# Chunk low parts moved from GpSimd to VectorE, and one more large product or two behind each phase's first count

## The chip, the core and the metric

The program runs on one core of a Trainium2 chip. Five engines work side by side, each through its own queue in order: TensorE (PE in the profile, with its weight loads as PEld), VectorE (DVE), ScalarE (ACT), GpSimd (POOL) and SyncE (SP, which only issues transfers here). They wait for one another through semaphores. The metric is the device time of one launch in microseconds; less is better. A difference of 0.2% (1.8 us) is about what a measurement of this kernel can tell from none.

## The reference

Three layers in a row: decayed causal attention over 4 x 8 heads of 576 tokens, a leaky feed-forward layer over all 2304 tokens, and an expert layer in which each of 8 experts takes exactly 288 tokens. Which expert a token goes to is decided by a greedy walk over all 18432 logits, largest first. Cut to what matters here:

```python
# second layer
h = x @ w_in                      # 2304 x 512 by 512 x 2048
g = np.maximum(0.01 * h, h)
x = g @ w_out                     # "the second product": 2304 x 2048 by 2048 x 512
# third layer
logits = x @ w_gate               # 2304 x 8
order = np.argsort(-logits.flatten())
for idx in order:                 # a token takes the first expert in the order that has room
    tok, e = int(idx) // E, int(idx) % E
    if assigned[tok] >= 0 or counts[e] >= cap: continue
    assigned[tok] = e; counts[e] += 1
out[mask_e] = np.maximum(x[mask_e] @ w1[e], 0) @ w2[e]      # for each expert e
```

## The kernel before

The kernel runs in stages. The first 190 us or so are attention. Up to about 440 us TensorE makes the first product of the leaky layer, twice over half of its 2048 columns, and the gate's logits with it. From 440 us to 659 us two things share TensorE, and the change is there. From 659 us the rows of the first expert are gathered, and from 675 us the eight experts run.

**What shares TensorE from 440 us.** `deferred` (L976) is a generator that gives out the second product, one matmul at a time. It goes over nine groups `g` of 256 tokens; in a group over eight chunks, each of which is two 128-row blocks of the inner 2048. fp32 operands are split into a high and a low part, both read as fp32r, and a product is the sum of three matmuls: high by high, high by the weight's low part, low by high. A chunk is thus 12 matmuls of 128x128 by 128x512 ("large products" below), a group 96, all of it 864. `taken` (L990) fetches a chunk, a tile `g1` that is still in SBUF or a tile `g0` read back from memory, and `split_g` (L454) makes the parts: `gh` is a cast on ScalarE (L458), `gl` a subtraction (L459). Each has three buffers, so ScalarE can write `gh` of a chunk once TensorE is through with the chunk three before it. For groups 0 to 7 `gl` is made on GpSimd; in the last group the first two chunks are on VectorE, and the rest on VectorE in a fixed order.

`routing` (L1256) is the greedy walk, done as a threshold search. It has seven phases of the same form, 0 to 6, and a last one that only assigns. In a phase VectorE first brings the state up to date and forms each token's wish `r_oh` (about twenty small instructions, L1391 to L1338, called the update below). Then five counts follow, three for the high digits of the threshold and two for the low ones. A count is: VectorE compares every token's key with 127 or 63 candidates (`r_ge`, L1358), TensorE adds up the results by expert (18 small matmuls into `q_ct`), VectorE reads them and marks which candidates hold (L1367, L1368: `r_found`), and TensorE sums the marks into the next base (`q_base`, one or more tiny matmuls), which the next `r_ge` reads as its scalar. After the counts, two small matmuls into `q_misc` give totals, and the next update begins.

**What sets the order.** TensorE's order is written out by the loop at L1119 to L1123. `routing` yields a number of nanoseconds each time that it has to wait for VectorE; the loop adds PACE (1.05) times that number to `slack` and lets `deferred` give out one large product for each 228 ns of it. `deal` later gives out the rest: up to the 852nd before the first expert's rows are turned (L1140), and the last 12 behind them. On TensorE everything stands in program order. On VectorE and ScalarE the instructions called by `V` and `A` are placed by a scheduler, those by `vec` and `act` stay in program order.

**The end of the stage.** When all is assigned, three groups of six small matmuls into `q_misc` (L1452) turn the assignment into row numbers `ids`. GpSimd then issues three indirect transfers that gather the first expert's rows (`xe`, L1034, 96 rows of 2 KB each). TensorE goes on with large products up to the 852nd, then turns the gathered rows by 36 small matmuls (L1143), 12 for each of the three gathers, into `q_ct`, `q_base` and `q_misc`. With the trace's 817 large products given out by the last of the three groups, 35 lie between it and the turning.

GpSimd has other work in that stage: per phase four small updates (L1406 to L1409), and for groups 3 and 4 the low parts of the first expert's weights (L988 through L366, printed as L75: `wh`, two instructions each time).

## Time and profile before

| | |
|---|---|
| median of 3 runs | 907.79 us (907.22 to 908.92) |
| the profiled execution | 908.27 us, of which the span of the instructions is 906.5 us |
| TensorE busy in the span | 879.0 us (97%) |
| VectorE / ScalarE / GpSimd busy | 583.2 / 413.1 / 439.1 us |
| granted TensorE clock, mean | 0.993 |

The page's busy times say which engine is the one that the others must keep fed; the waits say where it was not. A matmul's end is modelled, so a row's duration overlaps the next row: two large products that follow one another start 0.23 us apart though each is printed with 0.39 us. Where TensorE waits, the start of the waiting row tells more than the idle time printed beside it.

### The profile page before, as it was taken

Reading aid. Unit: us, or ns where it says so; the run is one execution under the profiler, and the core shown is the slowest. Engines: PE = TensorE matmul, PEld = TensorE weight load, DVE = VectorE, ACT = ScalarE, POOL = GpSimd, SP = SyncE. Lnnn points to the kernel's source line nnn. Section 1 sums busy time; section 2 is a strip of 40 time slices with the busy share of each in tenths; the row PEclk is TensorE's granted clock in tenths of the full one; section 3 lists DMA queues with packets and bytes.
Section 4 is the critical chain, followed back from the end, with each engine's and each line's share of the span. In section 5 each row is a group of like instructions: output and inputs, shape, how many; then the busy total and the mean of one; then the engine's idle time right before and its main releaser. Section 6 shows DMA issues by size and latency. Waiting matters only on the chain.

```text
span 906.5 us, 18991 instructions
## 1 busy us (share of the span) xinstructions
PE 879.0 (97%) x6916; PEld 749.3 (83%) x6916; DVE 583.2 (64%) x1456; ACT 413.1 (46%) x986; POOL 439.1 (48%) x670
## 2 busy tenths in 40 slices
PE   6899999999999999999999999999999999999996
PEld 5688888877778887777777777777789999999995
DVE  8778776617789369524576767767755666666651
ACT  7999999852223223323222222222244545554541
POOL 8488895456999158200464666565122122221111
PEclk9899999999999999999999999999999999999998
DMA  6556655559985484431121321111247666665521
GB/s 130 149 159 167 179 144 129 145 165 350 326 284 175 151 230 139 154 94 47 56 85 60 93 82 59 59 63 55 71 148 219 206 195 204 186 197 177 186 88 35
DMA packets 139964, 132.33 MB, mean 146 GB/s; under 512 B 68480, under 2 KB 106688, under 8 KB 139872
## 3 DMA queue, kind: packets, MB, share of 16 engines
q1 hardware_dynamic: 135600, 121.40, 44.1%
q0 software_dynamic: 3072, 9.44, 3.6%
q8 instruction: 54, 0.88, 0.4%
q10 hardware_dynamic: 1200, 0.30, 0.2%
q14 instruction: 38, 0.31, 0.1%
HBM read 99.84 MB, written 31.08 MB: 144 GB/s over the span
## 4 chain that ended last, share of the span: by engine, by line
PE 78%; POOL 8%; issue 4%; DVE 3%; ACT 3%; DMA 2%; POOLq 0%; SPq 0%; ACTq 0%; DVEq 0%
PE acc L1112 21%; PE acc L75 11%; PE h L75 11%; PE y L1197 10%; PE h L1184 9%; PE s L75 7%; PE T L75 3%; POOL wsq L75 3%; PE q_ct L1112 2%; ACT kept L75 2%; POOL ln L75 2%; DVE r_ge L1358 1%; POOL wst L75 1%; DMA w<-in_moe_w_in 1%; PE T L1204 1%
## 5 line engine op out<-in xcount | busy, mean ns | idle before, releaser
L1112 PE MATMUL acc<-wh,gh 128*128 128x512 f32 x568 | 184.5, 400 | 0.0
L459 POOL TENSOR_TENSOR gl<-g,gh 128x512 fp32r<-128x512 f32 x63 | 104.8, 1669 | 77.8 <-ACT gh L458 74.2
L1112 PEld LDWEIGHTS acc<-wh,gh 128*128 128x128 f32 x568 | 105.1, 189 | 18.6
L1112 PE MATMUL acc<-wh,gl 128*128 128x512 f32 x284 | 113.3, 399 | 0.0
L458 ACT CAST gh<-g 128x512 fp32r<-128x512 f32 x65 | 40.2, 621 | 145.8 <-PE acc L1112 135.6
L75 PE MATMUL acc<-X,wh 128*128 128x512 f32 (+1 forms) x480 | 104.6, 374 | 0.7 <-issue 0.7
L1197 PE MATMUL y<-eh,wh 128*128 128x288 f32 x512 | 104.3, 297 | 0.0
L75 PE MATMUL h<-X,wh 128*128 128x512 f32 (+1 forms) x480 | 104.3, 374 | 0.0
L1184 PE MATMUL h<-XE,wh 128*128 128x288 f32 x660 | 100.7, 299 | 0.0
L75 PEld LDWEIGHTS acc<-X,wh 128*128 128x128 f32 x480 | 82.5, 188 | 19.1 <-issue 2.1
L75 PEld LDWEIGHTS h<-X,wh 128*128 128x128 f32 x480 | 82.5, 188 | 17.5 <-issue 1.2
L1184 PEld LDWEIGHTS h<-XE,wh 128*128 128x128 f32 x660 | 89.8, 188 | 0.0
L75 ACT ACTIVATE kept<-kept,nm 128x192 f32<-128x192 f32 (+4 forms) x160 | 88.0, 553 | 3.1 <-DVE nm L75 3.1
L1210 POOL DMA_INDIRECT out<-yo,ids x24 | 22.5, 936 | 124.5 <-DVE yo L1206 98.3
L1197 PEld LDWEIGHTS y<-eh,wh 128*128 128x128 f32 x512 | 82.0, 188 | 0.0
L75 DVE TENSOR_TENSOR wh<-ws,wh 128x512 fp32r<-128x512 f32 x116 | 75.6, 687 | 2.5
L1189 DVE SCALAR_TENSOR_TENSOR el<-h,eh 128x288 fp32r<-128x288 f32 x64 | 29.2, 457 | 73.5 <-ACT eh L1188 73.5
L1197 PE MATMUL y<-el,wh 128*128 128x288 f32 x256 | 74.6, 297 | 0.0
L75 DVE SCALAR_TENSOR_TENSOR wbits<-w,wbits 128x256 int32<-128x256 int32 x128 | 72.6, 569 | 2.3
L75 DVE CUSTOM_DVE_ANT_0 kept<-s,mask 128x192 f32<-128x192 f32 (+4 forms) x160 | 59.2, 426 | 23.0 <-PE s L75 22.0
L75 POOL TENSOR_TENSOR wst<-wsq,wbits 128x256 f32<-128x256 f32 x64 | 50.6, 791 | 34.3 <-DVE wbits L75 29.6
L1188 ACT ACTIVATE eh<-h 128x288 fp32r<-128x288 f32 x64 | 26.3, 411 | 89.5 <-PE h L1184 77.6
(252 smaller groups left out, 1801.5 us busy)
## 6 DMA issues: line engine op xcount, KB each, us to landing
ws<-in_moe_w SPq DMA_DIRECT2D x116, 256.0 KB
X<-xd SPq DMA_DIRECT2D x12, 1024.0 KB
g<-gd SPq DMA_DIRECT2D x36, 256.0 KB
w<-in_moe_w_in SPq DMA_DIRECT2D x32, 256.0 KB
w<-in_moe_w_out SPq DMA_DIRECT2D x32, 256.0 KB
gd<-g SPq DMA_DIRECT2D x16, 512.0 KB
xd<-xt SPq DMA_DIRECT2D x16, 320.0 KB
x2d<-xo SPq DMA_DIRECT2D x20, 256.0 KB
```

The costliest lines, as they stand in the source:

```text
L75: r = getattr(self.engine, name)(*a, **k)
L458: hi_on.copy(gh, g)
L459: on.tensor_tensor(gl, g, gh, op=OP.subtract)
L1112: tc.keep_in_program_order(PE.matmul(*a, **k))
L1184: (pe if own else PE).matmul(h[:, :CAP], w[:, 128 * (j % 4):128 * (j % 4) + 128], X[:, c, x, :], start=n == 0, stop=n == 3 * NC - 1)
L1188: A.activation(gh, h[:, :CAP], AF.Relu)
L1189: V.scalar_tensor_tensor(gl, h[:, :CAP], 0.0, gh, op0=OP.max, op1=OP.subtract)
L1197: o = PE.matmul(yt[c][:, :CAP], w[:, s], a, start=j == 0 and n == 0, stop=j == NJ - 1 and n == 2)
L1204: PE.transpose(p[:M, 128 * c:128 * c + 128], ys[:, c, M * t:M * t + M], ident)
L1210: sd = G.indirect_dma_start(out=out[:, :], out_offset=bass.IndirectOffsetOnAxis(ap=ids[:, 3 * e + t:3 * e + t + 1], axis=0), in_=y, in_off ...
L1358: V.scalar_tensor_tensor(many[:, :NT * (K + 1)].rearrange("p (i k) -> p i k", k=K + 1)[:, :, :K], key[:, :, None].to_broadcast(s), base if ...
```

## The change

Two edits, of one line each. In `taken`, the low part `gl` of a chunk of groups 0 to 7 is called on `V` (VectorE, placed by the scheduler) instead of `G` (GpSimd); the last group is as before. In `routing`, the yield ahead of the first count's last base product (`half == n == 0`) grows from 550 to 850.

```diff
                 n = NF // 2 * half + i
-                return split_g(x, *((vec, act) if g == NG - 1 and n > 1 else (V if g == NG - 1 else G, A)))
+                return split_g(x, *((vec, act) if g == NG - 1 and n > 1 else (V, A)))
             ahead = begun if g == 0 else []
...
                 V.tensor_scalar(found[:, n:n + 1], most, 0.0, stp, op0=OP.is_ge, op1=OP.mult)
-                yield 550
+                yield 550 + 300 * (half == n == 0)
                 mm(base, rows[K], found[:, n:n + 1], start=n == 0, stop=True)
```

63 subtractions change engine. The 300 ns come once in each of seven phases: 300 x 1.05 / 228 = 1.38 large products each time, 9.7 in all. The count of large products given out by the last group of `q_misc` goes from 817 to 827, and so 25 instead of 35 are left up to the turning.

VectorE, the first count of phase 2 (`r_step_6152` are the 127 candidates; `g_...` is the chunk that is read). Before:

```order
L1336 TENSOR_TENSOR r_mw<-r_mw,r_U 128x18
L1358 SCALAR_TENSOR_TENSOR r_ge<-r_kf,r_step_6152 128x18x127
L1338 TENSOR_TENSOR r_oh<-r_mw,r_we 128x144
L1367 ISA r_jk,r_most<-q_ct,r_nr 128x8
L1367 ISA r_most 128x1
L1368 TENSOR_SCALAR r_found<-r_most 128x1
```

And in the changed kernel:

```order
L1336 TENSOR_TENSOR r_mw<-r_mw,r_U 128x18
L1358 SCALAR_TENSOR_TENSOR r_ge<-r_kf,r_step_6152 128x18x127
L459 TENSOR_TENSOR gl<-g_6944,gh 128x512
L1338 TENSOR_TENSOR r_oh<-r_mw,r_we 128x144
L459 TENSOR_TENSOR gl<-g_6988,gh 128x512
L459 TENSOR_TENSOR gl<-g_7033,gh 128x512
L1367 ISA r_jk,r_most<-q_ct,r_nr 128x8
```

Three low parts stand behind the 127-wide compare, ahead of the count's reading; a fourth stands in the update ahead of these rows. The first of the three, of chunk 21, is read by the 255th large product.

VectorE, the third count of phase 0 (`r_step_6156` are 63 candidates). Before:

```order
L1358 SCALAR_TENSOR_TENSOR r_ge<-r_kf,q_base,r_step_6156 128x18x63
L1367 ISA r_jk,r_most<-q_ct,r_nr 128x8
L1367 ISA r_most 128x1
L1368 TENSOR_SCALAR r_found<-r_most 128x1
L1374 TENSOR_SCALAR r_k_6367<-r_kf,q_base 128x18
```

And in the changed kernel:

```order
L1358 SCALAR_TENSOR_TENSOR r_ge<-r_kf,q_base,r_step_6156 128x18x63
L1367 ISA r_jk,r_most<-q_ct,r_nr 128x8
L1367 ISA r_most 128x1
L459 TENSOR_TENSOR gl<-g_6426,gh 128x512
L1368 TENSOR_SCALAR r_found<-r_most 128x1
L1374 TENSOR_SCALAR r_k_6369<-r_kf,q_base 128x18
```

A low part has come between the reading of the count and its mark, in this count alone.

GpSimd, one piece of the difference, from the small updates behind phase 1's counts to those behind phase 2's (`wh` are the weights' low parts):

```order
 L75 TENSOR_TENSOR wh<-wst,wh 128x512 x2
-L459 TENSOR_TENSOR gl<-g_5606,gh 128x512 x4
-L459 TENSOR_TENSOR gl<-g_7246,gh 128x512
-L1407 TENSOR_SCALAR r_nr<-r_rp 128x8
-L1408 TENSOR_SCALAR r_r<-r_rp 128x8
-L1409 TENSOR_TENSOR r_nr<-r_nr,r_r 128x8
-L1406 TENSOR_TENSOR r_A<-r_A,r_asg 128x144
-L459 TENSOR_TENSOR gl<-g_7285,gh 128x512
-L459 TENSOR_TENSOR gl<-g_7303,gh 128x512
-L459 TENSOR_TENSOR gl<-g_7370,gh 128x512
+L1406 TENSOR_TENSOR r_A<-r_A,r_asg 128x144
+L1407 TENSOR_SCALAR r_nr<-r_rp 128x8
```

The low parts are gone from GpSimd, and each pair of `wh` has moved up: before it stood among the low parts of a phase's counts, now between L1409 and L1406, that is in the update that leads to phase 2 (the second pair: to phase 3).

## Rows read from the trace of the kernel before

**Rows 1.** The page, busy time of an engine, share of the span, instructions.

```profile
PE 879.0 (97%) x6916; PEld 749.3 (83%) x6916; DVE 583.2 (64%) x1456; ACT 413.1 (46%) x986; POOL 439.1 (48%) x670
```

**Rows 2.** Stretch: length, busy of each engine, granted clock, DMA share, GB/s.

```profile
370.00:590.00 220.00, 218.01 (x1431) 164.86 (x1430) 130.91 (x292) 54.78 (x93) 93.18 (x91) 1.00 0.23 73
```

**Rows 3.** Waits of TensorE from 430 to 680 us: total, times, longest.

```profile
PE q_ct L1112 <- DVE r_ge L1358: 2.2, 6, 0.8
```

**Rows 4.** Groups by line, within 370 to 620 and 439 to 660 us.

```profile
L459 POOL TENSOR_TENSOR gl<-g,gh 128x512 fp32r<-128x512 f32 x57 | 95.3, 1678 | 68.1 <-ACT gh L458 64.9 <-DVE W L75 1.9 <-PE acc L1112 1.2
L1358 DVE SCALAR_TENSOR_TENSOR r_ge<-r_kf,q_base,r_step 128x1134 bf16<-128x1134 f32 x12 | 20.4, 1697 | 3.9 <-PE q_base L1112 3.9
L75 POOL TENSOR_TENSOR wh<-wst,wh 128x512 fp32r<-128x512 f32 x4 | 6.2, 1565 | 0.0
...
L75 DVE TENSOR_TENSOR gl<-g,gh 128x512 fp32r<-128x512 f32 x5 | 3.4, 687 | 0.9 <-ACT gh L75 0.9
```

**Rows 5.** Timeline, phase 2: start, duration, work, [idle before and releaser].

```profile
507.33 2.50 DVE L1358 SCALAR_TENSOR_TENSOR r_ge<-r_kf,q_base,r_step 128x1134 bf16<-128x1134 f32 x1 [0.35 <-PE q_base L1112]
...
508.85 0.63 PE L1112 MATMUL acc<-wh,gh 128*128 128x512 f32 x2
...
509.90 0.64 PE L1112 MATMUL q_ct<-r_oh,r_ge 128*128 128x8 bf16 x18 [0.42 <-DVE r_ge L1358]
...
510.94 1.29 POOL L459 TENSOR_TENSOR gl<-g,gh 128x512 fp32r<-128x512 f32 x1
...
511.20 2.23 DVE L1358 SCALAR_TENSOR_TENSOR r_ge<-r_kf,q_base,r_step 128x1134 bf16<-128x1134 f32 x1 [0.26 <-PE q_base L1112]
```

**Rows 6.** Timeline of VectorE, end of phase 2 and update to phase 3.

```profile
519.84 1.41 DVE L1358 SCALAR_TENSOR_TENSOR r_ge<-r_k,q_base,r_step 128x1134 bf16<-128x1134 f32 x1 [0.46 <-PE q_base L1112]
...
525.21 0.16 DVE L1391 TENSOR_TENSOR r_rp<-r_r,q_misc 128x8 f32<-128x8 f32 x1 [0.89 <-PE q_misc L1112]
525.41 0.54 DVE L1393 TENSOR_SCALAR r_pen<-r_rp 128x8 f32<-128x8 f32 x1
...
527.72 0.43 DVE L1346 TENSOR_TENSOR r_k<-r_m,r_k 128x18 int32<-128x18 int32 x1
...
528.72 0.68 DVE L1348 TENSOR_SCALAR r_k<-r_k 128x18 int32<-128x18 int32 x1
...
529.73 2.54 DVE L1358 SCALAR_TENSOR_TENSOR r_ge<-r_kf,r_step 128x2286 bf16<-128x2286 f32 x1
```

**Rows 7.** Timeline of TensorE, phase 3, behind the first count.

```profile
536.14 0.40 PE L1112 MATMUL acc<-wh,gl 128*128 128x512 f32 x1
536.54 0.16 PE L1112 MATMUL q_base<-r_found,r_rows 128*128 128x1 bf16 x1
```

**Rows 8.** Timeline from the last row-number matmuls to the turning.

```profile
658.61 0.41 PE L1112 MATMUL q_misc<-r_ge 128*96 128x48 bf16 x6
...
661.42 0.62 ACT L75 CAST gh<-g 128x512 fp32r<-128x512 f32 x1 [2.79 <-PE acc L1112]
...
662.68 2.49 DVE L75 TENSOR_TENSOR wh<-wst,wh 128x512 fp32r<-128x512 f32 x4
...
663.21 0.96 POOL L1034 DMA_INDIRECT xe<-x2d,ids  x1 [0.31 <-issue]
...
664.00 2.17 SPq L360 DMA_DIRECT2D wst<-in_moe_w  x4
...
668.64 0.61 PE L1112 MATMUL q_ct<-ident,xe 96*128 96x96 f32 x4
```

**Rows 9.** Issue to landing: the third gather alone, then nine gathers together.

```profile
DMA to landing us min/median/max: 3.7/3.7/3.7
...
DMA to landing us min/median/max: 3.1/6.4/7.6
```

**Rows 10.** Queues from 666.0 to 666.5 us: packets, MB, share of 16 engines.

```profile
q1 hardware_dynamic: 75, 0.15, 93.3%
q0 software_dynamic: 19, 0.02, 13.4%
```

## Prediction

> **What bounds the kernel now.** I read the page's busy times first: TensorE works 879.0 us of a span of 906.5 [rows 1], so only what it does not do, or waits for, can be won. [...] No engine but TensorE is short of time there, and the change can give back at most TensorE's waits in the stage. The waits view names them: six times `q_ct`, the sums of a count, waits for `r_ge`, 2.2 us in all, 0.8 at the longest [rows 3]. The timeline tells more than that column. One large product is printed with 0.40 us and two in a row with 0.63 [rows 5, 7], so they start 0.23 us apart. The two that start at 508.85 are through at 509.31, and `q_ct` starts at 509.90 [rows 5]: 0.59 us lost where 0.42 is printed, since a product's modelled end lies 0.17 us behind its share of the cadence.

> Why `r_ge` is late is in the same rows. Undisturbed it takes 1.41 us [rows 6]. At 511.20 it took 2.23: GpSimd's `gl` had started at 510.94 and ended at 512.23, and 1.41 us from there is almost to the end of `r_ge` [rows 5]. The 2.50 at 507.33 is the same thing. The groups agree: the 63-wide `r_ge` has a mean of 1697 ns, and `gl`, 1290 ns in that row, a mean of 1678 on GpSimd [rows 4, 5]. Each engine stands still while the other has its instruction.

> **The change part by part.** The base is the profiled execution, 908.27 us, 0.48 above the median of 907.79.

> *Removed, the six waits.* 2.2 us by the waits view and 0.17 more for each by the cadence: 3.2 us. With no `gl` on GpSimd in the counts, `r_ge` falls to about 1.41 us, which the large products dealt behind each count cover. I take it whole; 2.2 is the lower end.

> *Moved, 63 low parts.* On VectorE one costs 0.69 us, as five did in the last group [rows 4]; 63 x 0.69 = 43 us. VectorE has 220 - 131 = 89 us free in the stretch alone [rows 2], and gets back what `r_ge` is stretched now, 12 x (1.70 - 1.41) = 3.5 us for the plain ones alone. Almost all stand behind an `r_ge` and ahead of the count's reading (L1367), where VectorE waits for TensorE's eighteen matmuls anyway (0.64 us for the eighteen, behind its own wait) [rows 5]. Cost: nothing. If that cover were gone, each would make TensorE wait up to 0.69 us. Two places have no such cover.

> *Added, phase 0's third count.* Here `gl` stands between L1367 and L1368, so the mark comes 0.69 us later. Two large products are dealt there, and at 536.14 two were 0.17 us too few already [rows 7]. I take 0.6, with ends of 0 (the two cover more here) and 0.7.

> *Added, the weights' low parts in two updates.* The pairs of `wh` on GpSimd now run in the update that leads to phase 2, and in that to phase 3. The first low part that TensorE needs behind it is chunk 21's, read by the 255th large product; 213 are given out when the update's totals are there, so 41 lie between: 41 x 0.23 = 9.4 us. VectorE's way to it: from L1391 at 525.21 to `r_ge` at 529.73 is 4.52 us, of which three small instructions, at 0.16 each as at L1391, are stretched to 0.54, 0.43 and 0.68, 1.17 in all, by GpSimd's work, so 3.35 undisturbed [rows 6]. To it come one `gl` in the update (0.69), the 127-wide `r_ge` (2.54), the chunk's own `gl` (0.69) and 0.26 us from a release to the start [rows 5]: 7.5 us, 1.9 to spare. Against that stand two instructions of GpSimd, which stop VectorE. From below, one that runs 1.29 costs the overtaken 0.82 [rows 5], so 1.6 for two, and nothing is late. From above, two at the printed mean of 1565 ns [rows 4], 3.1, and TensorE waits 1.2 us at each place. The update is a chain of small instructions, of which none can pass the one that is stopped, so I take 2.5, close to two full 1.29: 0.6 late, 1.2 for both (0 to 2.4). [...]

> *Second edit, first counts.* By phase 3, 2, 3, 2, 3, 3 and 2 large products stand between the mark and `q_base`; now 4, 4, 4, 4, 3, 4 and 4. Where there are two, as at 536.14, `q_base` comes 0.40 us behind the last one's start, not 0.23 [rows 7]. Three times 0.17 is 0.5 us gained. Where there are three, nothing is waited for today, so nothing is gained, and the products are only moved.

> *Second edit, the tail.* What is given out earlier is missing later: 25 large products instead of 35 between the row numbers and the turning, so the turning comes 10 x 0.23 = 2.3 us sooner after them. The third gather is issued at 663.21 and lands 3.7 us later, at 666.91 [rows 8, 9]. Its turning starts at 668.64 [rows 8], its weight load some 0.1 before; moved up that is 666.2: 0.7 us late by an unchanged landing. But the landing may not stay. The weights' transfers of SyncE begin at 664.00, released by VectorE's `wh` at 662.68, which stands behind ScalarE's `gh` at 661.42, and that waits for a large product [rows 8]. With ten more done by then they start earlier, over the gather. At 666.0 to 666.5 those hold 93.3% of the transfer engines and the gathers' queue 13.4% [rows 10]. The ends: 3.1 us of landing, the least among nine gathers, gives 0.1, the median 6.4 gives 3.4, the greatest 7.6 gives 4.6 [rows 9]. The traced 3.7 had already some of that load over its last us, so I stay near it: 1.2 us.

> **Sum:** -3.2 - 0.5 + 0.6 + 1.2 + 1.2 = -0.7 us. 908.27 - 0.7 = 907.6 for an execution like the profiled one, 907.1 by the median. Behind the turning every engine's order is unchanged, and so is the time.

> **The rivals.** *Faster:* the updates hide the `wh` pairs (1.6 us and less of stretch) and the gather lands as before. Then -3.7 + 0.6 + 0.7 = -2.4 us, 905.4; without phase 0's price and the tail's, -3.7, 904.1. For it speaks that GpSimd, without the low parts, has little left to disturb; against it that the pairs were among the counts and are now in a chain.

> *Slower:* the third gather is held up by the weights' transfers. The price is the landing less 3.0 us of cover, and the rest of the sum is -1.9; it decides from a wait of 3.7 us on, a landing of 6.7. At the 7.6 of the nine gathers, 4.6 - 1.9 = +2.7, 910.5. For it speaks the 93.3% against 13.4%; against it that those nine gathers had one another for company, and this one only the loads of 1 MB. [...]

> *Slower, VectorE becomes late:* if in each of seven phases a low part stood ahead of a needed mark, 7 x 0.69 = 4.8 us would be added instead of phase 0's 0.6: +3.5, 911.3. The order shows one such place, so it has little.

> *The change doesn't do what it says:* `r_ge` stays late because of the updates of state that GpSimd keeps, or the large products, now fed by VectorE, wait as often. Then the 3.2 are not gained, and -0.5 with phase 0's 0.6 and the tail's 0.7 make +0.8, 908.6: no change that a measurement can tell. It tells about 0.2% (1.8 us) from none.

> **How the numbers follow.** The forecast, -0.7 with its terms as taken, has 0.47; the faster rival 0.28; the change without effect 0.10; the held gather 0.10; VectorE late 0.05. The first and the fourth hold the cases within 0.2%: 0.57. Faster by more than that is 0.28, slower 0.15. The range leaves out the best of the faster case (below 904.5) and the worst of the slower ones (above 909.9, which is a landing near 7 us): some 0.1 on either side.

> **What would show it.** Right: no row of `q_ct` waiting for `r_ge` in the stage, the 63-wide `r_ge` at 1.4 us, `gl` on VectorE at 0.69, `q_base` no more than 0.24 behind a large product at the first counts, a wait for `gl` of chunks 21 and 30 of about 0.6 us, and one before the third turning of 1 us. The last row-number matmuls should then start 10 x 0.23 - 3.7 + 1.8 = 0.4 us later than at 658.61 [rows 8]. Wrong: `gl` on VectorE well over 0.69, large products that wait for `gl` in most chunks, a turning that waits over 3 us, or one that doesn't wait though it comes 2 us sooner.

## The result and the profile of the changed kernel

The changed kernel takes 913.72 us (median of 5 runs, 913.17 to 914.62), beside 908.92 (907.22 to 909.72) for the kernel before in as many: a ratio of 1.0069, 95% interval 1.0054 to 1.0084. It is slower by 0.7%, where I had forecast 907.1 and no change that can be told. The time lies above the range.

Three landmarks of the traces cut the loss in two. The first is the first large product that reads a `gh`; the second is `ids`, the row numbers on VectorE; the third is the first `h`, the first expert's first product on TensorE. The stretches between their starts, in us:

| | before | changed |
|---|---|---|
| first large product to `ids` | 216.70 (442.57 to 659.27) | 216.74 (442.00 to 658.74) |
| large products given out by the last row-number matmuls | 817 | 827 |
| `ids` to the first `h` | 15.55 (to 674.82) | 20.65 (to 679.38) |
| first `h` to the last instruction of an engine | 226.94 | 226.94 |

Ten products are 2.3 us (10 x 0.23), and the stage up to `ids` made them in the same time, so it gained 2.3 us, more than I had forecast. The stretch behind it, the tail, should have become 15.55 - 2.3 = 13.25 us and took 20.65. All of the loss, 7.4 us, is there.

The waits of TensorE from 430 to 690 us in the changed kernel (total, times, longest), which answer to [rows 3]:

```profile
PE q_ct L1112 <- DMA xe<-x2d,ids: 3.9, 1, 3.9
PE acc L1112 <- DVE gl L459: 0.5, 2, 0.3
PE q_base L1112 <- DVE r_found L1368: 0.3, 1, 0.3
```

The six waits for `r_ge` are gone. Two waits for `gl` and one for `r_found` are new, and they are the small ones. The large one stands ahead of the turning. The groups of the stage, 440 to 659 us (busy us, mean ns | idle), which answer to [rows 4]:

```profile
L459 DVE TENSOR_TENSOR gl<-g,gh 128x512 fp32r<-128x512 f32 x65 | 45.0, 702 | 6.4 <-ACT gh L458 6.0
L1358 DVE SCALAR_TENSOR_TENSOR r_ge<-r_kf,q_base,r_step 128x1134 bf16<-128x1134 f32 x14 | 19.7, 1406 | 5.6 <-PE q_base L1112 5.6
```

The 63-wide compare is back at its undisturbed 1.41 us, and a low part costs 0.70 on VectorE. The two places that I had priced show as foreseen. First TensorE at phase 0's third count, then the chunk behind the update to phase 2, then VectorE and GpSimd in that update (start, duration, work, idle before and its releaser):

```profile
455.28 0.39 PE L1112 MATMUL acc<-wh,gh 128*128 128x512 f32 x1
456.00 0.16 PE L1112 MATMUL q_base<-r_found,r_rows 128*128 128x1 bf16 x1 [0.33 <-DVE r_found L1368]
```

```profile
505.11 0.61 PE L1112 MATMUL acc<-wh,gh 128*128 128x512 f32 x2
506.00 0.50 PE L1112 MATMUL acc<-wh,gl 128*128 128x512 f32 x1 [0.27 <-DVE gl L459]
```

```profile
497.76 1.78 DVE L459 TENSOR_TENSOR gl<-g,gh 128x512 fp32r<-128x512 f32 x1
499.46 1.40 DVE L1332 TENSOR_TENSOR r_eq<-r_W,r_m 128x144 f32<-128x144 f32 x1
```

```profile
497.63 3.07 POOL L75 TENSOR_TENSOR wh<-wst,wh 128x512 fp32r<-128x512 f32 x2
```

By the cadence of 0.23 us the count lost 456.00 - 455.51 = 0.49 us, and the chunk 506.00 - 505.57 = 0.43 and 0.11 more at the next product; the other update reads the same. In the update the `gl` that should take 0.69 takes 1.78, and `r_eq`, a small instruction of 0.30, takes 1.40, both while GpSimd has its two `wh`. Added up over all large products of the stage (every gap between a large product's start and the next start, less 0.227, where more than 0.1 is left), TensorE lost 3.99 us in 11 places before and loses 1.55 in 5 now.

Now the tail. Before, GpSimd and VectorE behind `ids`:

```profile
659.37 0.64 DVE L75 TENSOR_SCALAR XE<-xe,r_df 128x288 fp32r<-128x288 f32 x2
...
659.76 1.92 POOL L1034 DMA_INDIRECT xe<-x2d,ids  x1 [14.70 <-DVE ids L75]
...
659.93 0.68 DVE L75 TENSOR_TENSOR gl<-g,gh 128x512 fp32r<-128x512 f32 x1
...
662.07 0.69 DVE L75 TENSOR_TENSOR gl<-g,gh 128x512 fp32r<-128x512 f32 x1 [1.47 <-ACT gh L75]
```

and in the changed kernel, with what follows on the other engines:

```profile
658.27 0.62 ACT L75 CAST gh<-g 128x512 fp32r<-128x512 f32 x1 [2.77 <-PE acc L1112]
...
658.84 0.64 DVE L75 TENSOR_SCALAR XE<-xe,r_df 128x288 fp32r<-128x288 f32 x2
...
659.22 4.92 POOL L1034 DMA_INDIRECT xe<-x2d,ids  x1 [14.63 <-DVE ids L75]
...
659.39 1.28 DVE L75 TENSOR_TENSOR gl<-g,gh 128x512 fp32r<-128x512 f32 x2
...
660.59 2.49 DVE L75 TENSOR_TENSOR wh<-wst,wh 128x512 fp32r<-128x512 f32 x4
...
661.90 2.01 SPq L360 DMA_DIRECT2D wst<-in_moe_w  x4
...
664.44 0.93 POOL L1034 DMA_INDIRECT xe<-x2d,ids  x1 [0.30 <-issue]
665.67 0.92 POOL L1034 DMA_INDIRECT xe<-x2d,ids  x1 [0.30 <-issue]
668.14 0.61 PEld L1112 LDWEIGHTS q_ct<-ident,xe 96*128 96x128 f32 x4 [4.32 <-DMA xe<-x2d,ids]
```

The first gather occupies GpSimd for 4.92 us instead of 1.92. Before, VectorE had a gap behind its first `gl`, since ScalarE's `gh` of the last chunk waited for a large product until 661.42 [rows 8]; the gather ended 1.07 us behind that `gl`. Now the ten products are done earlier, `gh` runs at 658.27, and VectorE has the two marks (short compares, the rows `XE<-xe,r_df`), two `gl` and four `wh` in one piece up to 663.08; the gather ends at 664.14, 1.06 us behind its end. The other two gathers queue behind it, and TensorE stands for 4 us. Behind the wait the clock falls (length, busy of each engine, granted clock, DMA share, GB/s):

```profile
666.00:668.00 2.00, 0.00 (x0) 0.00 (x0) 0.00 (x0) 0.00 (x0) 0.59 (x1) 1.00 1.03 294
668.00:670.00 2.00, 1.86 (x10) 1.86 (x11) 0.00 (x0) 0.00 (x0) 0.00 (x0) 0.63 0.29 79
670.00:672.00 2.00, 2.00 (x12) 2.00 (x11) 0.00 (x0) 0.00 (x0) 0.00 (x0) 0.50 0.00 0
```

The granted clock is 0.63 of full speed from 668 to 670 us and 0.50 from 670 to 674, where it is 1.00 in the kernel before. From the first turning to the first `h` it is 679.38 - 668.14 = 11.24 us, against 674.82 - 666.89 = 7.93 before: the clock costs 3.3 us. Wait (4.1 by the cadence, from 0.23 behind the start of the last large product at 663.85 to 668.14) and clock make the 7.4.

### The profile page after: what moved, and what is told of

It reads as the page before. It is cut to its first block, busy times and chain, and to the rows that moved or that the text cites. A ratio compares the mean times of both kernels' runs of the same rounds, so it can differ in the third digit from the quotient of the medians.

```text
span 911.4 us, 19000 instructions
## 1 busy us (share of the span) xinstructions
PE 880.7 (97%) x6916; PEld 750.5 (82%) x6916; DVE 603.1 (66%) x1519; ACT 412.5 (45%) x986; POOL 335.9 (37%) x607
## 4 chain that ended last, share of the span: by engine, by line
PE 78%; POOL 6%; issue 4%; ACT 4%; DVE 3%; DMA 3%; SPq 1%; POOLq 0%; DVEq 0%; ACTq 0%
PE acc L1112 21%; PE acc L75 11%; PE y L1197 10%; PE h L75 10%; PE h L1184 9%; PE s L75 8%; PE T L75 3%; ACT kept L75 3%; PE q_ct L1112 2%; POOL wsq L75 2%; POOL wst L75 1%; POOL ln L75 1%; DVE kept L75 1%; PE T L1204 1%; DMA xe<-x2d,ids 1%
## 5 line engine op out<-in xcount | busy, mean ns | idle before, releaser
L75 ACT CAST wh<-ws 128x512 fp32r<-128x512 f32 x116 | 66.4, 618 | 0.0
L1112 PEld LDWEIGHTS acc<-wh,gl 128*128 128x128 f32 x284 | 53.9, 190 | 11.0 <-DVE gl L459 1.4
```

The costliest lines, as they stand in the source:

```text
L75: r = getattr(self.engine, name)(*a, **k)
L1112: tc.keep_in_program_order(PE.matmul(*a, **k))
```

## The experiments

Theory A, formed on these rows: the second edit makes the loss, by letting VectorE's work run in one piece over the first gather. The rivals are named with each run. In the table, "stage" is from the first large product to `ids`, "tail" from `ids` to the first `h`, both in us from one trace each; ratios are to runs of the kernel before beside them.

| kernel | median us | ratio, interval | stage | products | tail | first gather us |
|---|---|---|---|---|---|---|
| before | | | 216.70 | 817 | 15.55 | 1.92 |
| both edits (the change) | 913.72 | 1.0069 (1.0054 to 1.0084) | 216.74 | 827 | 20.65 | 4.92 |
| e1 low parts only | 906.55 | 0.9993 (0.9981 to 1.0004) | 215.31 | 817 | 15.55 | 1.91 |
| e2 yield only | 913.32 | 1.0066 (1.0049 to 1.0083) | 215.43 | 827 | 21.20 | 4.92 |
| e3 both, updates shorter | 906.97 | 0.9998 (0.9989 to 1.0007) | 215.86 | 817 | 15.55 | 1.91 |
| e4 both, gate | 906.02 | 0.9983 (0.9972 to 0.9995) | 216.73 | 827 | 13.85 | 2.52 |
| e5 yield, gate | 904.60 | 0.9967 (0.9951 to 0.9983) | 216.21 | 827 | 13.92 | 2.52 |
| e6 both, products first | 910.55 | 1.0031 (1.0016 to 1.0047) | 216.74 | 827 | 17.58 | 4.92 |
| e7 both, early gather | 913.52 | 1.0065 (1.0046 to 1.0083) | 216.75 | 827 | 21.66 | 4.69 |
| e8 both, marks behind | 908.76 (one) | | 216.74 | 827 | 17.05 | 1.35 |
| e9 both, loads behind | 911.37 | 1.0039 (1.0023 to 1.0055) | 216.74 | 827 | 19.39 | 4.93 |
| e10 yield, gate, marks early | 903.08 | 0.9953 (0.9939 to 0.9966) | 215.39 | 827 | 13.27 | 1.35 |
| e11 both, two-input marks | 915.11 | 1.0078 (1.0059 to 1.0097) | 216.74 | 827 | 21.32 | 5.10 |
| e12 both, wait filled | 910.73 | 1.0037 (1.0021 to 1.0053) | 216.78 | 827 | 18.13 | 4.92 |
| e13 both, marks read another tile | 915.48 (one) | | 216.73 | 827 | 22.34 | 4.92 |
| e14 both, marks after one low part | 910.87 (one) | | 216.72 | 827 | 18.13 | 1.35 |
| e15 both, marks signal apart | 922.04 (one) | | 216.73 | 827 | 26.56 | 4.92 |
| e16 as e10, with the first edit | 906.09 | 0.9987 (0.9976 to 0.9997) | 216.68 | 827 | 13.27 | 1.35 |

### Which edit makes the loss

**e1**, the first edit alone:

```diff
-                return split_g(x, *((vec, act) if g == NG - 1 and n > 1 else (V if g == NG - 1 else G, A)))
+                return split_g(x, *((vec, act) if g == NG - 1 and n > 1 else (V, A)))
```

> The first edit alone: the 63 low parts on VectorE, every yield as before, so 817 large products are out when the row numbers are made, and 35 are left up to the turning. Theory A (the loss is made by the second edit: with ten products done earlier, ScalarE's and VectorE's work on the last chunk and on the weights runs right behind the row numbers without a gap, and the first gather on GpSimd can't get through until that stream ends): first gather near the 1.92 us of before, no wait ahead of the turning, clock 1.00 throughout 660 to 680 us, and 1.5 to 3 us faster than before. Theory B (the first edit makes it: GpSimd, idle now between the updates, is slow at its first gather): first gather near 4.9 us, a wait of 3 to 4 us ahead of the turning, 3 to 5 us slower.

The tail is that of before to 0.01 us, with a first gather of 1.91. Theory B falls. The gain is smaller than I said: 1.4 us by the trace, and within the interval none. TensorE's losses go from 3.99 to 2.81 us only, because the place of the `r_ge` waits is taken by another:

```profile
PE q_base L1112 <- DVE r_found L1368: 0.9, 3, 0.3
```

In the two largest losses (0.5 us each by the cadence) a low part runs between the reading of a count and its mark (`gl` from 512.32 and from 538.27), as in phase 0's third count of the changed kernel.

**e2**, the second edit alone:

```diff
-                yield 550
+                yield 550 + 300 * (half == n == 0)
```

> The second edit alone: low parts on GpSimd as before, 300 ns more at each phase's first count. Theory A: first gather 4 to 5 us, a wait of 3 to 4 us ahead of the turning, a stretch at the lower clock behind it, and 5 to 7 us slower than before, so slower than both edits together by 1 to 3 us. Theory B: first gather near 1.9 us, at most 1 us of wait ahead of the turning, and within 1 us of before.

```profile
657.37 4.92 POOL L1034 DMA_INDIRECT xe<-x2d,ids  x1 [14.43 <-DVE ids L75]
```

A first gather of 4.92 us, the wait (3.9) and the clock (0.50 from 668 to 672 us): theory A holds in the tail, and the second edit alone makes it. The stage is the surprise, and with it the time, which is that of both edits and not 1 to 3 us more. With the low parts still on GpSimd, it gains 216.70 - 215.43 + 2.3 = 3.6 us, and of 3.99 us lost in 11 places 0.23 are left in one. The compares and the low parts in that stage:

```profile
L1358 DVE SCALAR_TENSOR_TENSOR r_ge<-r_kf,q_base,r_step 128x1134 bf16<-128x1134 f32 x14 | 21.3, 1524 | 6.4 <-PE q_base L1112 6.4
...
L1358 DVE SCALAR_TENSOR_TENSOR r_ge<-r_k,q_base,r_step 128x1134 bf16<-128x1134 f32 x7 | 9.9, 1407 | 2.8 <-PE q_base L1112 2.8
...
L459 POOL TENSOR_TENSOR gl<-g,gh 128x512 fp32r<-128x512 f32 x62 | 102.9, 1661 | 75.0 <-ACT gh L458 72.1 <-DVE W L75 1.9 <-PE acc L1112 0.8
```

GpSimd still runs 62 low parts of 1.66 us, but they meet the compares less: of the two forms of the 63-wide `r_ge` one has a mean of 1.52 and the other of 1.41 us, where the same stretch of the kernel before has 1.66 and 1.59:

```profile
L1358 DVE SCALAR_TENSOR_TENSOR r_ge<-r_kf,q_base,r_step 128x1134 bf16<-128x1134 f32 x14 | 23.2, 1656 | 4.7 <-PE q_base L1112 4.7
```

A low part starts when ScalarE's `gh` is done (72.1 us of GpSimd's idle time ends so), and `gh` waits for TensorE (in the kernel before, 135.6 of ScalarE's 145.8 us of idle time ahead of it end so), so other places for the large products move the low parts against the compares. That this is why they now miss each other is argued, not shown. Nor is it the same each time: e5 and e10 below have this stage too, and took 216.21 us with 1.01 us lost and 215.39 us with 0.21.

**e3**, both edits, and the products taken back once in each phase:

```diff
-        yield 6700
+        yield 6400
```

> Both edits, and the yield of each update is 6400 instead of 6700, so the 300 ns are taken back once in each phase: 817 products out and 35 left, as before. Theory A: first gather near 1.9 us, no wait ahead of the turning, 2 to 3.5 us faster than before and 7 to 8 us faster than the changed kernel. Theory B: the tail of the changed kernel again, 4 to 5 us slower than before. If the updates need the products that were taken from them, TensorE waits for the first count's r_ge or for gl, some 1 us in each of seven phases.

With 35 products in the tail the first gather takes 1.91 us and the tail 15.55. What the time lost in the change came from the ten products, and theory B falls again. But the stage gave up most of its gain: 3.18 us are lost in 11 places, nearly all ahead of a `q_base`, as with the first edit alone. Whether the products taken from the updates are missed there or the low parts, dealt otherwise, stand worse, this run doesn't tell apart. No gain can be told in the time.

### Is it VectorE's work that holds the gather, and what does each part of the tail cost

**e4**, both edits, and a tiny copy ahead of the four `wh` that waits for the first gather's rows (the gate):

```diff
                         if g == NG - 1 and len(ahead) == NF:
+                            vec.tensor_copy(junk, ax[:M, 0, :1])
                             for m in (2, 3):
...
+        junk = cst.tile([96, 1], FT, name="junk")
```

> Both edits; ahead of VectorE's four low parts of the weights in the tail stands one tiny copy that reads the first gather's rows, so the four, and the weights' loads that wait for them, come behind that gather's landing. The large products are as in the changed kernel, 25 up to the turning. Theory A: the first gather shrinks from 4.92 us to 2 to 2.6 us, the wait ahead of the turning from 3.9 us to 0 to 1.5, and the time to 0.5 to 2.5 us under that of before. Theory C (ten products less are too little cover whatever VectorE does): the first gather may shrink, but a wait of 2 us or more and the lower clock stay, and the time stays over that of before.

```profile
660.19 2.52 POOL L1035 DMA_INDIRECT xe<-x2d,ids  x1 [14.63 <-DVE ids L75]
663.00 0.93 POOL L1035 DMA_INDIRECT xe<-x2d,ids  x1 [0.30 <-issue]
```

VectorE's work without the `wh` ended 1.45 us behind the gather's start, and the gather 1.07 behind that. ScalarE's four casts of `wh` stand as early there as in the changed kernel (659.77 to 661.95), so it isn't they that hold the gather. No wait is left ahead of the first turning, the clock stays at 1.00 from 660 to 680 us, and the tail is 13.85: 0.6 over 13.25, since the second and third turning start as their rows land, 0.2 and 0.3 us late by e10's spacing. Theory C falls: 25 products are cover enough but for that.

**e9**, both edits, with the loads of 1 MB kept behind the third gather by a tiny operation of GpSimd that reads the two weight tiles:

```diff
+        raws.append(st)
...
                                 early.extend(split_weights(piece(0, m), vec, act))
+                                gp.tensor_tensor(junk, ax[:M, 2, :1], raws[-1][:M, :1], op=OP.add)
```

> Both edits; a tiny operation of GpSimd, which waits for the third gather's rows, also reads the two weight tiles, so the loads of 1 MB into them begin behind that gather and not at its side. VectorE's order is that of the changed kernel, so the first gather should be held for 4.9 us as there. If the loads slow the landing: the first gather lands 2.1 us behind its end, as before the change, instead of 3.9; the wait ahead of the turning is 1.5 to 2.5 us instead of 3.9, and h starts 1.5 to 2.5 us earlier, unless the later loads are missed there. If they don't: 3.9 us of wait as in the changed kernel.

The first gather's time from issue to landing, before, in the changed kernel and here:

```profile
xe<-x2d,ids POOLq DMA_INDIRECT x1, 4.0
```

```profile
xe<-x2d,ids POOLq DMA_INDIRECT x1, 8.9
```

```profile
xe<-x2d,ids POOLq DMA_INDIRECT x1, 7.0
```

Of the 4.9 us that the first gather lands later, 3.0 are GpSimd's (4.92 - 1.92) and 1.9 are the loads at its side. That is the transfer that my slower rival named, but it is the smaller part. The wait ahead of the turning shrinks by 1.9, to 2.0 us, and the tail by 1.3 alone: the clock falls here too, to 0.50 from 668 to 674 us, and the second and third turning start as their rows land, 0.5 and 0.2 us late by e10's spacing.

**e6**, both edits, with all large products ahead of the turning:

```diff
-        deal(96 * NG - 12)
+        deal(96 * NG)
```

> Both edits; the last 12 large products stand ahead of the turning instead of behind it, so 37 cover the gather and not 25. The first gather should be held as in the changed kernel (4.9 us). Theory K (the lower clock behind the wait comes from the wait's length): the wait shrinks from 3.9 us to about 1.2, the clock stays at 1.00, and the kernel gains 2.7 + 3.3 = 6 us on the changed one, so it ends 0 to 2 us under the time of before. Theory L (the clock falls with any wait there, or of itself): the clock falls behind the turning all the same, and it gains only the 2.7 us.

```profile
668.15 0.69 PE L1112 MATMUL q_ct<-ident,xe 96*128 96x96 f32 x4 [1.75 <-DMA xe<-x2d,ids]
```

```profile
668.00:670.00 2.00, 1.85 (x16) 1.85 (x17) 0.00 (x0) 0.37 (x1) 0.00 (x0) 0.96 0.09 29
670.00:672.00 2.00, 2.00 (x11) 2.00 (x11) 0.00 (x0) 0.00 (x0) 0.00 (x0) 0.50 0.69 262
```

The wait is 1.8 us and not 1.2, the lower clock comes all the same (0.50 from 670 to 676 us), and the tail gains 3.1 us: theory L is the nearer one. A clock of 0.50 stood here behind 1.8 us of wait, and not only behind 4.

**e12**, both edits, and the wait filled:

```diff
         deal(96 * NG - 12)
+        fa, fb = wo0[-1]["w"][1]
+        for _ in range(17):
+            mm(px[0], fa[:, :128], fb, start=True, stop=True)
```

> Both edits, and 17 matmuls of the large products' size, whose result is overwritten, between the last of the 25 and the turning: 17 x 0.23 = 3.9 us, just the wait. The gathers are not touched. If the lower clock behind the wait is caused by TensorE standing still: the clock stays at 1.00, h starts 17.0 to 17.6 us behind the row numbers instead of 20.65, and the kernel is 3.3 us faster than the changed one (about 1.8 us over before). If the clock falls for another reason, the time is that of the changed kernel.

```profile
668.00:670.00 2.00, 1.25 (x11) 0.97 (x9) 0.00 (x0) 0.00 (x0) 0.00 (x0) 1.00 0.67 164
670.00:672.00 2.00, 2.00 (x17) 2.00 (x18) 0.00 (x0) 0.00 (x0) 0.00 (x0) 1.00 0.00 0
```

The gather is held as in the changed kernel, the clock stays at 1.00 from 658 to 682 us, though 0.7 us of wait are left, and the tail is 2.5 us shorter; without that 0.7 it would be 3.2, about the 3.3 that I read from the rows. So standing still is what costs TensorE its clock here.

**e5**, the second edit and the gate, low parts on GpSimd:

```diff
+                            vec.tensor_copy(junk, ax[:M, 0, :1])
...
-                yield 550
+                yield 550 + 300 * (half == n == 0)
```

> The second edit alone (low parts on GpSimd, as before the change), with the tiny copy ahead of VectorE's four low parts of the weights that waits for the first gather. Theory A: stage as with the second edit alone (3.5 us less waited for than before), first gather 2.5 us, 0.6 us lost in the tail, together 2.5 to 3.5 us faster than before, and faster than both edits with the copy by about 1 us. If the weights' low parts, which come later here, are missed by the first expert, its first product starts more than 14 us behind the row numbers and the gain is gone.

As expected in the tail: 2.52 us for the first gather and 13.92 in all. The kernel is 0.33% faster than before. The stage, in the order of e2, is 0.8 us longer than there; one place, a `q_ct` that waits for `r_ge`, lost 0.81.

### What about that work holds it

**e7**, both edits, with an early gather, so that the first expert's is not the first one of the program:

```diff
+        zi, zo = cst.tile([96, 1], I32, name="zi"), cst.tile([96, 8], FT, name="zo")
+        G.tensor_scalar(zi, where[0][:M, 0:1], 0.0, None, op0=OP.mult)
+        G.indirect_dma_start(out=zo, out_offset=None, in_=w_gate[:, :], in_offset=bass.IndirectOffsetOnAxis(ap=zi[:, 0:1], axis=0))
```

> Both edits; GpSimd makes one more gather, of 96 rows of 32 bytes from the gate's weights, some us ahead of the first expert's, so that this is not the first one of the program. Theory A (VectorE's stream holds the gather): the first gather of the expert's rows still takes 4.9 us and the time is that of the changed kernel, 4 to 6 us over before. Theory F (the first gather of a program is slow of itself, and VectorE's stream only happens to be there): it takes about 1 us, the wait ahead of the turning is under 1.5 us, and the time is 1 to 3 us under before.

4.69 us instead of 4.92, and the same loss. Being the first one of the program costs 0.23 us; theory F falls.

**e8**, both edits, with the two marks (`sel8`, printed as `XE<-xe,r_df`) moved from ahead of the two `gl` to behind the turning in the program, which puts them behind the four `wh`:

```diff
-        for t in range(2):
-            vec.tensor_scalar(sel8[t], ax[:, 3, :CAP], where[0][:, NT - 2 + t:NT - 1 + t], None, op0=OP.is_equal)
         gather(0, [ax[:M, t] for t in range(3)])
...
+        for t in range(2):
+            vec.tensor_scalar(sel8[t], ax[:, 3, :CAP], where[0][:, NT - 2 + t:NT - 1 + t], None, op0=OP.is_equal)
         deal(96 * NG)
```

> Both edits; the two short instructions of VectorE that make the marks of the last 288 tokens, which stand between the row numbers and the last two low parts, stand behind the weights' low parts instead. VectorE's stream behind the row numbers is then six subtractions of two inputs alone. Theory A: the first gather is held to the end of that stream and takes 4.2 to 4.4 us, 0.6 less than 4.92. Theory M (only an instruction like the marks, with one input and a scalar, takes from GpSimd what it needs): it takes 1 to 1.5 us.

```profile
658.08 1.28 DVE L75 TENSOR_TENSOR gl<-g,gh 128x512 fp32r<-128x512 f32 x2
...
658.46 1.35 POOL L1034 DMA_INDIRECT xe<-x2d,ids  x1 [14.63 <-DVE ids L75]
659.28 2.49 DVE L75 TENSOR_TENSOR wh<-wst,wh 128x512 fp32r<-128x512 f32 x4
660.12 1.25 POOL L1034 DMA_INDIRECT xe<-x2d,ids  x1 [0.30 <-issue]
```

Theory A as I had put it falls. VectorE's six subtractions run in one piece, and two gathers get through beside them, each only after the instruction that ran when it began (the first `gl` ends 0.29 behind the gather's start, and 0.29 + 1.06 = 1.35). The tail is still 17.05, by waits of 0.3 and 1.4 us for the second and third gather, which land beside the loads (the third 5.5 us behind its issue, 3.7 before), and by the lower clock behind them (0.50 from 668 to 670 us). This and the other kernels with one run each are read by their traces, not by their times.

**e11**, both edits, the marks in their place, by an operation with two tensors as inputs:

```diff
-            vec.tensor_scalar(sel8[t], ax[:, 3, :CAP], where[0][:, NT - 2 + t:NT - 1 + t], None, op0=OP.is_equal)
+            vec.tensor_tensor(sel8[t], ax[:, 3, :CAP], where[0][:, NT - 2 + t:NT - 1 + t].to_broadcast([128, CAP]), op=OP.is_equal)
```

> Both edits; the two marks stay where they are, at the first gather's start, but are made by an operation with two tensors as inputs (the place of a token repeated along the row) instead of one tensor and a scalar. Theory M (the form of the instruction that runs as the gather begins is what holds it): first gather 1.0 to 1.6 us, a wait of 1 to 2 us in the tail as with the marks behind, and 3 to 4 us less than the changed kernel. Theory P (the place of the marks is what counts, whatever their form): first gather 4.9 us and the time of the changed kernel.

5.10 us, held up to the end of the piece. Theory M falls: the form of the marks isn't it.

**e13**, both edits, the marks reading another tile than the one that the gathers write, and **e15**, both edits, each mark with a signal of its own through a tiny transfer of SyncE.

```diff
+        io2 = g1p.tile([128, CAP], FT, name="io2", tag="g1b", bufs=1)
-        G.iota(ax[:, 3, :CAP], ...)
+        G.iota(io2, pattern=[[1, CAP]], base=0, channel_multiplier=0, allow_small_or_imprecise_dtypes=True)
-            vec.tensor_scalar(sel8[t], ax[:, 3, :CAP], where[0][:, NT - 2 + t:NT - 1 + t], None, op0=OP.is_equal)
+            vec.tensor_scalar(sel8[t], io2, where[0][:, NT - 2 + t:NT - 1 + t], None, op0=OP.is_equal)
```

```diff
+        scr = [drp.tile([96, 1], FT, name=f"scr{t}") for t in range(2)]
...
             vec.tensor_scalar(sel8[t], ax[:, 3, :CAP], where[0][:, NT - 2 + t:NT - 1 + t], None, op0=OP.is_equal)
+            nc.sync.dma_start(scr[t], sel8[t][:M, :1].bitcast(FT))
```

> Both edits; the two marks stay where they are, but compare with a row of numbers that lies in another tile, and not in the one into which the gathers write. Theory T (the gather is held because VectorE still reads the tile that it writes into): first gather 1.0 to 1.6 us. Theory P (the marks' place decides, not what they read): 4.9 us, to the end of VectorE's stream and 1.06 us more.

> Both edits; each of the two marks signals its own end, because a tiny transfer of SyncE reads each; in the changed kernel the first signals nothing and the second adds two to VectorE's count. Place and operands are those of the changed kernel. Theory S (the joint signal is what holds the gather): first gather 1.0 to 1.6 us. Theory P: 4.9 us.

4.92 us in both. Neither the tile nor the signal is it. (In e15 the tail is far longer, 26.56 us, with a wait of 8.5 us; that run was made for the gather's own duration.)

**e14**, both edits, the marks between the two `gl`:

```diff
+                        if g == NG - 1 and len(ahead) == NF - 1:
+                            for t in range(2):
+                                vec.tensor_scalar(sel8[t], ax[:, 3, :CAP], where[0][:, NT - 2 + t:NT - 1 + t], None, op0=OP.is_equal)
                         ahead.append(taken(len(ahead) // (NF // 2), len(ahead) % (NF // 2)))
...
-        for t in range(2):
-            vec.tensor_scalar(sel8[t], ax[:, 3, :CAP], where[0][:, NT - 2 + t:NT - 1 + t], None, op0=OP.is_equal)
```

> Both edits; the marks stand between the last two low parts of the chunks instead of ahead of both, so the gather begins while a low part runs and the marks follow at once. VectorE's stream is as long as in the changed kernel. Theory P1 (what VectorE runs as the gather begins decides): first gather 1.35 us, as with the marks behind. Theory P2 (marks anywhere in the stream ahead of the weights' low parts hold it): 4.3 us or more.

```profile
659.22 1.35 POOL L1037 DMA_INDIRECT xe<-x2d,ids  x1 [14.64 <-DVE ids L75]
659.44 0.64 DVE L75 TENSOR_SCALAR XE<-xe,r_df 128x288 fp32r<-128x288 f32 x2
660.00 0.68 DVE L75 TENSOR_TENSOR gl<-g,gh 128x512 fp32r<-128x512 f32 x1
660.60 2.49 DVE L75 TENSOR_TENSOR wh<-wst,wh 128x512 fp32r<-128x512 f32 x4
660.88 3.01 POOL L1037 DMA_INDIRECT xe<-x2d,ids  x1 [0.30 <-issue]
```

The first gather gets through (1.35), but the second, which began beside a `wh`, takes 3.01 us: the four `wh` end at 663.09, and the gather 0.80 behind them. So P1 is right for the first gather, and yet the marks aren't needed for a gather to be held. Over the gathers and scatters of these traces that began beside a VectorE instruction with the next one right behind it (147), 132 ended 0.8 us or less (1.06 for the first of a program) behind the end of that one instruction, and 15 were held until VectorE paused. 14 of the 15 began beside a mark, the other is this one. The 14 are one event, the expert's first gather in 14 kernels, and they share another thing: each began 0.02 to 0.11 us into the instruction that ran, where 131 of the 132 began 0.15 us or more into it and one 0.07. So the mark and the moment at which the gather begins aren't told apart, and this one, 0.28 us into a `wh`, fits neither. I found no rule that tells the two cases apart; it stays open.

### The version that follows

**e10**, the second edit, the gate, and the marks made as soon as the places of the tokens are known:

```diff
+            if where and ax is None:
+                ax = g1p.tile([128, 4, 512], FT, name="xe", tag="g1a", bufs=1)
+                ...
+                for t in range(2):
+                    vec.tensor_scalar(sel8[t], ax[:, 3, :CAP], where[0][:, NT - 2 + t:NT - 1 + t], None, op0=OP.is_equal)
...
```

> As the kernel with the second edit and the gate (low parts on GpSimd; the weights' low parts wait for the first gather), and the two marks are made when the token's places are known, some 10 us ahead of the row numbers, so that no instruction of theirs runs as the first gather begins. Theory M (the gather is held when it begins at the side of such an instruction, up to the next gap in VectorE's stream): the first gather takes 1.2 to 1.5 us instead of 2.5, nothing waits in the tail, the first expert's h starts 13.3 to 13.6 us behind the row numbers, and the kernel is 3 to 4.5 us faster than before. Theory A (any stream of VectorE holds it): 2.5 us and 13.9 us as without this edit.

```profile
657.30 1.35 POOL L1035 DMA_INDIRECT xe<-x2d,ids  x1 [14.44 <-DVE ids L75]
658.96 0.93 POOL L1035 DMA_INDIRECT xe<-x2d,ids  x1 [0.30 <-issue]
660.19 0.92 POOL L1035 DMA_INDIRECT xe<-x2d,ids  x1 [0.31 <-issue]
660.77 0.15 DVE L75 COPY junk<-xe 96x1 f32<-96x1 f32 x1 [2.58 <-DMA xe<-x2d,ids]
660.85 2.48 DVE L75 TENSOR_TENSOR wh<-wst,wh 128x512 fp32r<-128x512 f32 x4
662.15 2.01 SPq L360 DMA_DIRECT2D wst<-in_moe_w  x4
```

All three gathers have begun on GpSimd before VectorE's `wh` and SyncE's loads begin; the waits view names none for TensorE from 430 to 690 us. The tail is 13.27 us, what 25 products should leave, and the kernel is 0.47% faster than before (0.34 to 0.61): faster than both kernels of this case.

**e16**, the same with the first edit added:

```diff
-                return split_g(x, *((vec, act) if g == NG - 1 and n > 1 else (V if g == NG - 1 else G, A)))
+                return split_g(x, *((vec, act) if g == NG - 1 and n > 1 else (V, A)))
```

> Both edits, marks early and the gate, that is, the fastest kernel so far with the first edit added. The tail should be that kernel's (first gather 1.35 us, no wait, clock 1.00), so the difference is what the first edit is worth when the tail is mended. If the stage's waits carry over from the traces (1.55 us with both edits, 0.2 to 1.0 with the second alone), it is 0.5 to 1.3 us slower than that kernel and 2.5 to 3.5 us faster than before; if the low parts on VectorE are worth what I forecast for them, it is faster than that kernel by 1 us or more.

The tails are equal, so up to the first `h` the two differ in the stage alone: 216.68 against 215.39. With the second edit there, the first costs 1.3 us by these two traces, and 0.5 by e5's 216.21. It removes the 0.2 us that is left and adds phase 0's `gl` (0.49) and the two updates (0.54 each). By the ratios, 0.9987 against 0.9953, it is 3.1 us slower (an estimate from the two intervals: 1.5 to 4.6), more than I had expected; what of that the stage doesn't explain stays open.

## Why the prediction was wrong, point by point

- **The bound** held. TensorE had 3.99 us of losses in the stage and nothing else to give; no kernel got more than 3.8 of them.
- **The waits removed and added in the stage** were sized well for both edits together. I had -3.7 and +1.8, that is -1.9; the losses fell by 2.4. Phase 0's count cost 0.49 (0.6 in the sum), each update 0.54 (0.6 in the sum), at the places named: in the updates a `gl` of 1.78 and an `r_eq` of 1.40 beside GpSimd's `wh`.
- **Who removes them** was wrong, so it is in part luck that the stage's sum came out near. I gave 3.2 us to the first edit and 0.5 to the second. The first alone lowers the losses by 1.2, the second alone by 3.0 to 3.8 (e5, e2, e10), and both together by 2.4. "Cost: nothing" for the 63 moved low parts fails for the first edit alone: there they stand ahead of `r_found` in more places (three waits, 0.9 us). With both edits it held, and the 1.55 that is left is the two places that I had priced by themselves.
- **The tail** is the step that made the forecast wrong. I took 1.2 us with ends of 0.1 and 4.6, and it was 7.4, of which 4.1 are wait. I had moved the turning up and asked when the third gather lands by an unchanged issue. It did land 4.2 us behind its issue, near the 3.7 that I took, but its issue went from 3.9 to 6.9 us behind `ids`, and TensorE waited for the first gather already. I had read that ScalarE's `gh` waits for a large product and that `wh` and the loads follow [rows 8], and that they would come earlier; I followed them to the transfer engines and not to GpSimd, where VectorE's work and the gather's issue meet. The traced 1.92 us of the first gather, twice the 0.93 of the second, was in the trace and I didn't ask why. The sign that I had named for being wrong, a turning that waits over 3 us, is there: 3.9.
- **The clock** was in no term. I priced a wait by its length; here a wait of 4 us cost 3.3 more in the stretch behind it.
- **The slower rival** had the place and the sign, and the bound of 3.7 us from which it decides was passed. Its cause, the weights' loads, is 1.9 us of the first gather's delay, beside 3.0 on GpSimd. It had a chance of 0.10, and its worst time of 910.5 lacked the hold and the clock.

## What to carry to other kernels

Work that is done earlier releases other work earlier: follow each released chain to everything that it shares with the next transfer on the critical path, the engine that issues the transfer among it, and ask of every traced duration that is twice its neighbour's why it is. Price a wait of TensorE with the clock behind it, from a stretch that shows both clocks (here 1.00 and 0.50). And where two edits go after the same waits, run each alone: here one of them was worth more without the other, and its price lay in another stage, where a gate of one tiny copy gave it back.
